# Stage one of two sequences with the two parts of x as rows, other ticks for the transforms, and two loads cut in the passage

## The chip, the cores and the metric

The kernel runs on one core of one Trainium2 chip. The metric is the device time of one execution in microseconds (us), smaller is better. The kernel before takes 1383.81 us, the median of three runs (1381.85 to 1385.62).

The names of the engines: PE is TensorE (PEld its weight loads), DVE is VectorE, ACT is ScalarE, POOL is GpSimd, SP is SyncE, which here only issues DMAs. Each engine runs its own instructions strictly in the order in which they stand.

## The reference

x has 4 sequences of 3008 rows of 256 columns. The Fourier transform runs along the 3008.

```python
X = np.fft.rfft(x, axis=1)
Yr = X.real @ w_r - X.imag @ w_i + b_r
Yi = X.real @ w_i + X.imag @ w_r + b_i
Yr = np.sign(Yr) * np.maximum(np.abs(Yr) - 0.01, 0.0)      # Yi likewise
y = np.fft.irfft(Yr + 1j * Yi, n=3008, axis=1)
h = y.reshape(12032, 256) @ w_in                           # 256 -> 2048
g = h / (1.0 + np.exp(-h))                                 # h * sigmoid(h)
out = g @ w_out                                            # 2048 -> 256
```

## The kernel before

3008 is 47 times 64, so each transform is two short ones. *Stage one* (`s1...`) takes 47 points: x is read as 94 rows by 32 columns of D=256, a row p being n2 and the upper or lower half of n1 together (p = 2·n2 + half), and a table of 94 x 96 is multiplied with it. Its result goes to a scratch tensor in DRAM (`scr1`). *Stage two* (`s2`, `s2_3`) takes the 64 points, then come the mix with w_r and w_i (`mix`, `mix3`, `shrink`), the first inverse stage (`split_z`, `i1`), a second scratch tensor (`scr2`), its reload (`g_load`, tile `gin`), and the second inverse stage (`i2`, `i2_ends`), which writes `xt`, the input of the MLP. The MLP's tokens go in 24 blocks (23 of 512 and one of 256).

A product of full precision is made of three products of the type fp32r, which holds fewer bits: a value is split into a high part (a cast on ACT) and a low part (value minus high part, on DVE), and high·high, high·low and low·high are added in PSUM. So stage one of the third and fourth sequence (`s1_half`, line 225) has three products of 512 columns for each half of a group of 1024 columns, and 8 groups for each sequence.

The first sequence, stage one of the second, and part of the splitting of w_in and w_out run ahead of the MLP: the *prologue*. Its last part, from the last inverse stage of sequence one to the first MLP products, is called the *passage* here. Then follow 384 *ticks*, one for each block and each 128 of the 2048 inner columns. Tick t issues, in this order: the split of the previous tick's g (`split_g`: ACT L512, DVE L513), a deferred `shrink`, the first product of tick t (`mlp1`: six matmuls, L495; then ACT sigmoid L502 and DVE product L503), then whatever was put into tick t (`fill`), then DMA stores, then the second product of tick t-2 (`mlp2`: eight matmuls, L535 and L539). The ticks 0 to 7 belong to block 0, 8 to 23 to block 1.

What is put where is decided when the program is written out: `put(t, ...)` takes the first free tick from t on, and `at(t, ...)` any tick. Stage two to i1 of a sequence is cut into pieces (`u3_step`), which take their ticks first, then stage one takes what is free. `W_GO[t]` is the number of steps that tick t does on the splitting of the MLP's weights; there are three kinds of step, which follow one another: two DVE operations L597 and L598, two DVE operations L604 and L605 (with ACT L601 and the beginning of the next weight, L595), two DVE operations L608 and L609. A split of x (`s1_split`) is put with `at`, its product with `put` in a later tick.

In the table below a tile's name is written without its number; `x_sb` and `x_pre` hold x, `sx` its split, `s1o` stage one's result, `d` is a pair of PSUM banks that all the products of the fills share in turn.

Of the kernel before, what the change touches and what calls it, by code (L numbers as in the profile page):

```python
# [100 lines left out]
def spectral_mlp_kernel(ctx: ExitStack, tc: tile.TileContext, x, w_r, w_i, b_r, b_i, w_in, w_out, c1, c2, c3, c4, c3f, out):  # L101
# [110 lines left out]
    def s1_split(b, g, i):  # L212
        t = x_t[b, g][:NP, i * 512:(i + 1) * 512]
        sx = sb.tile([128, 2, 512], F32R, tag="sx", bufs=1, name="sx")
        nc.scalar.copy(sx[:NP, 0, :], t)
        nc.vector.tensor_sub(sx[:NP, 1, :], t, sx[:NP, 0, :])  # L216
        x_t[b, g, i] = sx

    def s1_half(b, g, i):
        sx = x_t.pop((b, g, i))  # L220
        if i == 0:
            x_t[b, g, "o"] = sb.tile([128, 4 * D], F32, tag="s1o", bufs=2, name="s1o")[:96, :]
        o = x_t[b, g, "o"]
        p = bank("s1")
        s1_product(p, (sx[:, 0, :], sx[:, 1, :]))
        nc.scalar.copy(o[:, i * 512:(i + 1) * 512], p[:96, :])
        if i == 0:
            s1_split(b, g, 1)
        else:
            v = scr1[b].rearrange("r (a j) d -> (r a) (j d)", a=4)  # L230
            store(v[:, g * 4 * D:(g + 1) * 4 * D], o)
            del x_t[b, g], x_t[b, g, "o"]
            x_ahead()
# [617 lines left out]
```

## Time and profile before

| | |
|---|---|
| median of the runs | 1383.81 us |
| the profiled execution | 1383.51 us |
| its span, from first to last instruction | 1381.5 us |
| mean granted clock of TensorE | 0.998 |
| busy: TensorE, VectorE, ScalarE, GpSimd | 99%, 64%, 51%, 7% of the span |
| TensorE idle on the chain of waits | 4 steps over 1 us: 3.7 and 3.0 us on loads, 1.7 us on a load, 1.3 us on VectorE |

A step of the chain of waits names the instruction that waited and what came last before it could run. TensorE's rows overlap one another, since matmuls are pipelined: what one costs is the distance from its start to the start of the next, not its duration.

### The profile page before, as it was taken

Reading aid. Unit: us, or ns where it says so; the run is one execution under the profiler, and the core shown is the slowest. Engines: PE = TensorE matmul, PEld = TensorE weight load, DVE = VectorE, ACT = ScalarE, POOL = GpSimd, SP = SyncE. Lnnn points to the kernel's source line nnn. Section 1 sums busy time; section 2 is a strip of 40 time slices with the busy share of each in tenths; the row PEclk is TensorE's granted clock in tenths of the full one; section 3 lists DMA queues with packets and bytes.
Section 4 is the critical chain, followed back from the end, with each engine's and each line's share of the span. In section 5 each row is a group of like instructions: output and inputs, shape, how many; then the busy total and the mean of one; then the engine's idle time right before and its main releaser. Section 6 shows DMA issues by size and latency. Waiting matters only on the chain.

```text
span 1381.5 us, 20358 instructions
## 1 busy us (share of the span) xinstructions
PE 1363.3 (99%) x7621; PEld 1168.3 (85%) x7621; DVE 888.2 (64%) x1517; ACT 705.5 (51%) x1386; POOL 98.8 (7%) x145
## 2 busy tenths in 40 slices
PE   8998999999999999999999999999999999999998
PEld 4976788888888888888888888888888888888888
DVE  3867979687655677767655577776654555455555
ACT  5445555555564555555454445454454444444444
POOL 2000012111000101111100011111000000000000
PEclk9999999999999999999999999999999999999999
DMA  8874334231423214333121022220210110011001
GB/s 263 268 226 144 93 88 119 76 97 32 123 76 101 58 43 107 89 94 81 50 73 54 20 77 60 75 81 25 61 32 12 27 39 10 18 27 39 0 16 24
DMA packets 69932, 103.51 MB, mean 75 GB/s; under 512 B 7306, under 2 KB 53002, under 8 KB 69834
## 3 DMA queue, kind: packets, MB, share of 16 engines
q1 hardware_dynamic: 58163, 79.07, 19.8%
q0 software_dynamic: 8096, 19.45, 5.4%
q10 hardware_dynamic: 3575, 3.70, 0.8%
q8 instruction: 60, 0.98, 0.3%
q14 instruction: 38, 0.31, 0.1%
HBM read 64.70 MB, written 37.49 MB: 74 GB/s over the span
## 4 chain that ended last, share of the span: by engine, by line
PE 94%; DMA 2%; DVE 2%; ACT 1%; issue 1%; SPq 0%; ACTq 0%; DVEq 0%
PE h L495 37%; PE acc L535 24%; PE acc L539 12%; PE mix L349 6%; PE i L438 3%; PE s L324 2%; PE mix L288 2%; PE s L173 2%; PE i L397 2%; PE s L189 1%; PE acc L530 1%; PE s L267 1%; PE i L394 1%; PE i2e L438 1%; DMA t3f<-in_c3f_dram 1%
## 5 line engine op out<-in xcount | busy, mean ns | idle before, releaser
L495 PE MATMUL h<-xt,win 128*128 128x512 f32 (+1 forms) x2304 | 585.5, 389 | 0.4 <-DVE g L503 0.2
L535 PE MATMUL acc<-wout,gh 128*128 128x512 f32 x1472 | 540.7, 401 | 0.0
L495 PEld LDWEIGHTS h<-xt,win 128*128 128x128 f32 x2304 | 401.7, 188 | 82.7 <-ACT xt L454 0.5
L502 ACT ACTIVATE g<-h 128x512 f32<-128x512 f32 (+1 forms) x385 | 226.1, 587 | 385.0 <-PE h L495 384.1
L503 DVE TENSOR_TENSOR g<-h,g 128x512 f32<-128x512 f32 (+1 forms) x385 | 261.0, 678 | 239.8 <-ACT g L502 236.5
L539 PE MATMUL acc<-wout,gl 128*128 128x256 f32 x1472 | 413.1, 281 | 1.3 <-DVE gl L513 1.3
L513 DVE TENSOR_TENSOR gl<-g,gh 128x512 fp32r<-128x512 f32 (+1 forms) x385 | 276.0, 717 | 169.2 <-ACT gh L512 165.0
L535 PEld LDWEIGHTS acc<-wout,gh 128*128 128x128 f32 x1472 | 277.6, 189 | 59.4 <-issue 0.5
L512 ACT CAST gh<-g 128x512 fp32r<-128x512 f32 (+1 forms) x385 | 235.3, 611 | 158.5 <-DVE g L503 155.9
L539 PEld LDWEIGHTS acc<-wout,gl 128*128 128x128 f32 x1472 | 278.6, 189 | 11.5 <-DVE gl L513 2.4
L356 POOL TENSOR_TENSOR q<-q,bias 128x256 f32<-128x256 f32 x36 | 26.4, 733 | 652.6 <-ACT q L355 652.6
L438 PEld LDWEIGHTS i<-c_sb,gin 96*128 96x128 f32 x420 | 54.9, 193 | 8.6 <-issue 4.3
L369 DVE TENSOR_TENSOR y<-q,mix 64x256 f32<-64x256 f32 x144 | 60.3, 419 | 2.2
L438 PE MATMUL i<-c_sb,gin 96*128 96x94 f32 x420 | 54.2, 274 | 3.3 <-DMA gin<-scr 3.3
L324 PEld LDWEIGHTS s<-t,a 128*128 128x128 f32 x288 | 37.7, 191 | 3.0
L324 PE MATMUL s<-t,a 128*128 128x128 f32 x288 | 37.9, 275 | 0.0
L455 DVE TENSOR_TENSOR xt<-i,xt 128x376 fp32r<-128x376 f32 (+2 forms) x48 | 28.0, 583 | 12.4 <-ACT xt L454 6.7
L173 PE MATMUL s<-sx,c 94*96 94x512 f32 (+1 forms) x111 | 34.1, 414 | 0.2 <-DVE sx L216 0.2
L397 PE MATMUL i<-zh,t 128*128 128x256 f32 x144 | 33.7, 297 | 0.0
L401 ACT COPY i1o<-i 128x512 f32<-128x512 f32 x48 | 27.8, 580 | 10.2 <-PE i L394 9.0
L556 DVE TENSOR_TENSOR o<-acc,o 128x256 f32<-128x256 f32 x92 | 32.6, 413 | 0.0
L357 POOL TENSOR_TENSOR q<-q,bias 128x256 f32<-128x256 f32 x36 | 31.9, 886 | 2.8
(118 smaller groups left out, 1164.7 us busy)
## 6 DMA issues: line engine op xcount, KB each, us to landing
a<-scr SPq DMA_DIRECT2D x48, 256.0 KB
gin<-scr SPq DMA_DIRECT2D x32, 384.0 KB
scr<-s1o SPq DMA_DIRECT2D x31, 384.0 KB
t<-in_c_dram POOLq DMA_DIRECT2D x36, 256.0 KB, 3.0
scr<-i1o SPq DMA_DIRECT2D x36, 256.0 KB
x_sb<-in_x_dram POOLq DMA_DIRECT2D x22, 376.0 KB, 4.1
t<-in_c_dram SPq DMA_DIRECT2D x48, 128.0 KB
w<-in_moe_w_in_dram SPq DMA_DIRECT2D x8, 512.0 KB
```

The source lines that it names most:

```text
L173: nc.tensor.matmul(out=p[:96, :], lhsT=c1_hl[m][:K, :], rhs=hl[k][:K, :], start=(n == 0), stop=(n == 2))
L324: nc.tensor.matmul(out=pv[:, e, :, r, :], lhsT=a[:, r, e * 128:(e + 1) * 128], rhs=t2[:, r * 128:(r + 1) * 128], start=True, stop=True,)
L349: nc.tensor.matmul(out=out, lhsT=x_[:, e, c, :], rhs=m[:, e, :], start=(n == 0), stop=(n == 5))
L397: nc.tensor.matmul(out=pv[:, r, :], lhsT=t3[:, m, q], rhs=z[k][:, r, :], start=(n == 0), stop=(n == 2),)
L438: nc.tensor.matmul(out=p[:, o:o + m], lhsT=g_t[b, j // 4][:, q:q + 128], rhs=c4_sb[:, p0:p0 + m], start=True, stop=True,)
L495: nc.tensor.matmul(out=p[:, :n], lhsT=w[:, e, f * 128:(f + 1) * 128], rhs=v[:, e, :n], start=(m == 0), stop=(m == 5),)
L502: nc.scalar.activation(out=g[:, q], in_=p[:, q], func=ACTF.Sigmoid)
L503: nc.vector.tensor_tensor(out=g[:, q], in0=p[:, q], in1=g[:, q], op=ALU.mult)
L512: nc.scalar.copy(gh[:, q], g[:, q])
L513: nc.vector.tensor_sub(gl[:, q], g[:, q], gh[:, q])
L535: nc.tensor.matmul(out=a, lhsT=gh[:, q], rhs=wout[:, f].rearrange("p a c -> p (a c)"), start=begins, stop=False,)
L539: nc.tensor.matmul(out=a[:, D:2 * D], lhsT=gl[:, q], rhs=wout[:, f, 0, :], start=False, stop=ends,)
```

## The change

Stage one of the sequences 2 and 3 (the third and fourth) is done another way. The two halves of n1 are taken apart, so that a piece of x has 47 rows (n2) and not 94, and there are 16 groups for each sequence and not 8. A piece is loaded twice, to the rows 0 to 46 and to the rows 64 to 110 of the same tile. The high part is cast over all 111 rows, and the rows from 64 on are replaced by the low part, so the two parts of x are rows of one operand. The new table c5 has its high part in the columns 0 to 63 and its low part in the columns 64 to 127, at both row ranges. One product then gives rows 0 to 63, the table's high part times both parts of x, and rows 64 to 127, the table's low part times both; ACT copies 48 of the lower rows out, and DVE adds the upper ones.

GpSimd loads c5 at tick 30, and the 64 loads of x where it issued 16. The splits and products get other ticks (third sequence from 54 on, every 2.8 ticks; fourth from 114 on, every 4.4), and so do the pieces of stage two to i1 (third from tick 104 every 4.3 instead of 92 every 5, fourth from 190 every 4.8 instead of 186 every 5). The last two products of stage one of the second sequence (`s1_later(7, ...)`) move from the ticks 2 and 4 to 6 and 7. `W_GO` does 13 steps in the ticks 0 to 7 where it did 11, the same as before in the ticks 8 to 18, and 5 instead of 7 after; the sum is 30 both times.

In the passage, the two loads of `gin` for block 0 are cut: 88 rows of each are issued one step of the pipeline earlier, after i1's last result but one, and 8 rows after the last one. The results of stage one for groups 4 and 5 of the second sequence go to two x tiles that nothing needs any more (later block 1's `xt`), so they don't wait for the two `s1o` buffers.

```diff
-W_GO = [2, 1, 1, 2, 1, 1, 2, 1, 0, 0, 0, 2, 1, 2, 1, 2, 1, 2, 1, 1, 2, 1, 2, 1]
+W_GO = [2, 2, 1, 2, 1, 2, 2, 1, 0, 0, 0, 2, 1, 2, 1, 2, 1, 2, 1, 2, 1, 1, 1]
...
+    def x_load_twice(b, q):
+        t = x_sb[q % 2]
+        if b == STACKED and q < 2:
+            nc.gpsimd.memset(t[32:64, :], 0.0)
+        h, g = divmod(q, 8)
+        v = x[b].rearrange("(n h j) d -> n h (j d)", h=2, j=NJ)[:, h, g * 4 * D:(g + 1) * 4 * D]
+        for p in (0, 64):
+            nc.gpsimd.dma_start(out=t[p:p + RR, :], in_=v)
+        return t
...
-    def s1_split(b, g, i):
...
-    def s1_half(b, g, i):
...
+    def stack_split(b, q):
+        t = x_t[b, q]
+        sx = sb.tile([128, 4 * D], F32R, tag="sx", bufs=1, name="sx")
+        nc.scalar.copy(sx[:64 + RR, :], t[:64 + RR, :])
+        nc.vector.tensor_sub(sx[64:64 + RR, :], t[64:64 + RR, :], sx[64:64 + RR, :])
+        x_t[b, q] = sx
+
+    def stack_product(b, q):
+        sx = x_t.pop((b, q))
+        o = sb.tile([128, 4 * D], F32, tag="s1o", bufs=2, name="s1o")[:2 * NR, :]
+        for i in range(2):
+            p = bank("s1")
+            c = slice(i * 512, (i + 1) * 512)
+            nc.tensor.matmul(out=p, lhsT=c5_sb[:64 + RR, :], rhs=sx[:64 + RR, c], start=True, stop=True)
+            nc.scalar.copy(o[:, c], p[64:64 + 2 * NR, :])
+            nc.vector.tensor_tensor(out=o[:, c], in0=p[:2 * NR, :], in1=o[:, c], op=ALU.add)
+        h, g = divmod(q, 8)
+        v = scr1[b].rearrange("r (i h j) d -> (r i) h (j d)", i=2, h=2)
+        store(v[:, h, g * 4 * D:(g + 1) * 4 * D], o)
+        x_ahead()
...
         s1(1, 2, late=True)
+        for g in range(2):
+            loaded.add((0, g))
+            g_load(0, g, slice(0, 88))
         flush(1)
         u_step(NU + 1)
         s1(1, 3, late=True)
-        i2_load(0)
-        flush(1)
+        for g in range(2):
+            g_load(0, g, slice(88, 96))
         s1(1, 4, late=True)
...
-            put(2, s1_later, 7, i)
+            put(5, s1_later, 7, i)
...
-        for b, t0, dt in ((2, 37, 6), (3, 110, 8)):
+        for b, t0, dt in ((2, 54, 2.8), (3, 114, 4.4)):
             t = 0
-            for g in range(8):
-                t = max(t, t0 + dt * g)
-                at(t, s1_split, b, g, 0)
-                t = put(t + 1, s1_half, b, g, 0)
-                t = put(t + 1, s1_half, b, g, 1)
+            for q in range(16):
+                t = max(t, int(t0 + dt * q))
+                at(t, stack_split, b, q)
+                t = put(t + 1, stack_product, b, q)
```

Three places where the order moves. First ScalarE in two ticks on end in stage one of the third sequence; before, one tick with a product and the split for the next one (`gh` begins a tick, the sigmoid `g` follows it):

```order
L512 CAST gh<-g 128x512 [waits DVE_49]
L502 ACTIVATE g<-h 128x512 [waits PE_49,Activation_49]
L226 COPY s1o<-s_2416 96x512 [waits PE_49]
L215 CAST sx<-x_sb_69 94x512 [waits DVE_49]
L512 CAST gh<-g 128x512 [waits DVE_49]
```

And in the changed kernel two such ticks on end, the ticks 68 and 69:

```order
L540 CAST gh<-g 128x512 [waits DVE_49]
L530 ACTIVATE g<-h 128x512 [waits PE_49,Activation_49]
L255 COPY s1o<-s_3725 48x512 [waits PE_49]
L255 COPY s1o<-s_3729 48x512 [waits PE_49]
L244 CAST sx<-x_sb_69 111x1024 [waits DMASW4_49,DMASW3_49,Activation_49]
L540 CAST gh<-g 128x512 [waits DVE_49]
L530 ACTIVATE g<-h 128x512 [waits PE_49,Activation_49]
L255 COPY s1o<-s_3765 48x512 [waits DMAHW7_49,PE_49]
L255 COPY s1o<-s_3769 48x512 [waits PE_49]
L244 CAST sx<-x_sb_70 111x1024 [waits DMASW6_49,DMASW5_49,DVE_49]
```

Between the sigmoid and the next `gh` stand three instructions where there were two, and the cast is of 1024 columns and not of 512. The product of the next tick needs this cast, and VectorE's subtraction behind it.

Second, TensorE in the ticks 1 and 2 (`i` is the second inverse stage of block 1, `h` mlp1, `acc` mlp2, `s` stage one). Before:

```order
L438 MATMUL i_1091<-c_sb,gin 128x94
L495 MATMUL h<-xt_1013,win_79 128x512 [waits DVE_49]
L495 MATMUL h<-xt_1013,win_80 128x512
L495 MATMUL h<-xt_1014,win_79 128x512
...
L205 MATMUL s_1123<-x_sb_69,c_sb 96x512 [waits DMAHW4_49,DMAHW3_49,PE_49]
L535 MATMUL acc<-wout,gh 128x512 [waits Activation_49]
L539 MATMUL acc<-wout,gl 128x256 [waits DVE_49]
```

In the changed kernel:

```order
L466 MATMUL i_1092<-c_sb,gin 128x94
L523 MATMUL h<-xt_1014,win_80 128x512 [waits DVE_49]
L523 MATMUL h<-xt_1014,win_81 128x512
L523 MATMUL h<-xt_1015,win_80 128x512
...
L563 MATMUL acc<-wout,gh 128x512 [waits Activation_49]
L567 MATMUL acc<-wout,gl 128x256 [waits DVE_49]
```

The product `s`, which waits for a load of x, is gone from tick 2 (it stands in tick 6), so mlp2 follows mlp1 and waits for VectorE's `gl` alone.

Third, SyncE's queue in the passage. Before:

```order
L142 DMA scr_1_83<-s1o 96x1024 [waits DMAHW0_49,Activation_49]
L409 DMA gin<-scr_0_86 96x1024 [waits DMAHW4_49,DMAHW2_49,DMAHW7_49,DMAHW1_49,DVE_49]
L409 DMA gin<-scr_0_86 96x1024 [waits DMAHW3_49,DVE_49]
L142 DMA scr_1_83<-s1o 96x1024 [waits Activation_49]
L579 DMA w_999<-in_moe_w_out_dram 128x2x512 [waits DMAHW5_49,DVE_49]
L142 DMA scr_1_83<-s1o 96x1024 [waits DMAHW6_49,Activation_49]
```

In the changed kernel:

```order
L438 DMA gin<-scr_0_87 88x1024 [waits DMAHW4_49,DMAHW0_49,DMAHW7_49,DVE_49,Activation_49]
L438 DMA gin<-scr_0_87 88x1024 [waits DMAHW2_49,DVE_49,Activation_49]
L157 DMA scr_1_84<-s1o 96x1024 [waits DMAHW3_49,Activation_49]
L438 DMA gin<-scr_0_87 8x1024 [waits DMAHW1_49]
L438 DMA gin<-scr_0_87 8x1024 [waits DMAHW5_49]
L607 DMA w_1000<-in_moe_w_out_dram 128x2x512 [waits DMAHW6_49,DVE_49]
L157 DMA scr_1_84<-s1o 96x1024 [waits Activation_49]
L157 DMA scr_1_84<-x_pre 96x1024 [waits DMAHW0_49,DMASW5_49,Activation_49]
```

The long loads stand ahead of a store of 96 rows, the two short ones behind it; two stores of stage one come behind the weights' load where one stood ahead of it.

## Rows read from the trace of the kernel before

**Rows 1.** The page's first part: busy us, share of span, instructions.

```profile
PE 1363.3 (99%) x7621; PEld 1168.3 (85%) x7621; DVE 888.2 (64%) x1517; ACT 705.5 (51%) x1386; POOL 98.8 (7%) x145
```

**Rows 2.** Windows: length, busy us (instructions) by engine, PE's granted clock, DMA share, GB/s.

```profile
95.00:98.50 3.50, 0.48 (x4) 0.39 (x4) 0.95 (x2) 0.12 (x1) 0.00 (x0) 1.00 0.91 263
98.50:102.00 3.50, 3.50 (x14) 2.41 (x14) 0.41 (x1) 1.52 (x3) 0.00 (x0) 0.53 0.80 316
...
111.00:115.50 4.50, 0.83 (x4) 0.43 (x3) 4.07 (x8) 2.29 (x4) 0.00 (x0) 1.00 0.47 111
115.50:119.50 4.00, 4.00 (x13) 3.21 (x12) 2.49 (x4) 1.10 (x2) 0.00 (x0) 0.57 0.39 132
...
181.00:700.00 519.00, 518.48 (x2985) 450.97 (x2984) 361.74 (x627) 281.72 (x565) 61.97 (x90) 1.00 0.29 81
```

**Rows 3.** Timeline of two ticks: start us, us, engine, line, operation [idle before].

```profile
522.99 0.86 PE L173 MATMUL s<-sx,c 94*96 94x512 f32 x3
...
523.69 0.40 PE L535 MATMUL acc<-wout,gh 128*128 128x512 f32 x1
...
525.08 1.55 PE L495 MATMUL h<-xt,win 128*128 128x512 f32 x6
...
526.47 0.39 PE L535 MATMUL acc<-wout,gh 128*128 128x512 f32 x1
...
526.73 0.60 ACT L502 ACTIVATE g<-h 128x512 f32<-128x512 f32 x1 [0.87 <-PE h L495]
...
527.36 0.69 DVE L503 TENSOR_TENSOR g<-h,g 128x512 f32<-128x512 f32 x1 [0.78 <-ACT g L502]
...
527.86 1.55 PE L495 MATMUL h<-xt,win 128*128 128x512 f32 x6
```

**Rows 4.** Timeline of a tick with a split of x, ScalarE.

```profile
533.92 0.60 ACT L502 ACTIVATE g<-h 128x512 f32<-128x512 f32 x1 [0.30 <-PE h L495]
...
534.42 0.61 ACT L215 CAST sx<-x_sb 94x512 fp32r<-94x512 f32 x1
```

**Rows 5.** Groups by shape, ScalarE: count, busy us, mean ns, idle before.

```profile
L226 ACT COPY s1o<-s 96x512 f32<-96x512 f32 x32 | 18.6, 582 | 2.5 <-PE s L173 0.5
...
L623 ACT ACTIVATE x_pre<-x_pre 64x1024 uint32<-64x1024 uint32 x2 | 2.0, 1036 | 0.0
```

**Rows 6.** Groups by shape, VectorE.

```profile
L216 DVE TENSOR_TENSOR sx<-x_sb,sx 94x512 fp32r<-94x512 f32 x32 | 22.4, 699 | 10.2 <-ACT sx L215 10.0
...
L503 DVE TENSOR_TENSOR g<-h,g 128x256 f32<-128x256 f32 x15 | 6.4, 424 | 2.2 <-ACT g L502 0.7
```

**Rows 7.** Who ScalarE's L475 (end of `i2_ends`) waits for: us, times.

```profile
  DVE xt L473: 20.1, 23
```

**Rows 8.** Timeline of the passage and the ticks 0 to 2.

```profile
90.62 0.37 ACTq L138 DMA_DIRECT2D scr<-i1o  x1
...
93.57 0.80 SPq L409 DMA_DIRECT2D gin<-scr  x2
...
98.14 1.27 PE L438 MATMUL i<-c_sb,gin 96*128 96x94 f32 x7 [3.02 <-DMA gin<-scr]
...
108.64 0.69 DVE L503 TENSOR_TENSOR g<-h,g 128x512 f32<-128x512 f32 x1 [0.58 <-ACT g L502]
...
109.25 0.68 DVE L608 TENSOR_TENSOR ww<-ww,wout 128x512 f32<-128x512 f32 x1
...
110.58 0.42 DVE L597 TENSOR_SCALAR ww<-ww 128x512 uint32<-128x512 uint32 x1
...
111.64 0.68 DVE L513 TENSOR_TENSOR gl<-g,gh 128x512 fp32r<-128x512 f32 x1
...
114.73 1.07 PE L205 MATMUL s<-x_sb,c_sb 128*96 128x512 f32 x2 [3.67 <-DMA x_sb<-in_x_dram]
...
115.23 0.91 PE L535 MATMUL acc<-wout,gh 128*128 128x512 f32 x1
```

**Rows 9.** Timeline, TensorE at the start of tick 11.

```profile
143.01 1.32 PE L495 MATMUL h<-xt,win 128*128 128x512 f32 x5
```

**Rows 10.** Loads of x issued by GpSimd (L158, 376 KB each).

```profile
DMA to landing us min/median/max: 3.5/4.8/10.8
```

More of the change, by code (lines that the diff above doesn't have):

```diff
@@ L90, in dft_tables @@
     c3f = c3
+    c, s = trig(np.outer(n2, r), RR)
+    c5 = np.zeros((128, 2, KK))
+    c5[:RR, 0, :2 * NR] = np.stack([c, -s], axis=2).reshape(RR, 2 * NR)
+    c5[:, :, 1] = 0.0
+    c5 = c5.astype(np.float32)
+    bits = c5[:RR, 0].view(np.uint32).astype(np.uint64)
+    c5h = ((bits + 0x7FF + ((bits >> 12) & 1)) & 0xFFFFF000).astype(np.uint32).view(np.float32)
+    c5[:RR, 1] = c5[:RR, 0] - c5h
+    c5[:RR, 0] = c5h
+    c5[64:64 + RR] = c5[:RR]
     return {
@@ L96, in dft_tables, with spectral_mlp_kernel @@
         "c3f": c3f,
+        "c5": c5.reshape(128, 128),
     }
 @with_exitstack
-def spectral_mlp_kernel(ctx: ExitStack, tc: tile.TileContext, x, w_r, w_i, b_r, b_i, w_in, w_out, c1, c2, c3, c4, c3f, out):
+def spectral_mlp_kernel(ctx: ExitStack, tc: tile.TileContext, x, w_r, w_i, b_r, b_i, w_in, w_out, c1, c2, c3, c4, c3f, c5, out):
     nc = tc.nc
@@ L111, in spectral_mlp_kernel @@
     c4_sb = cst.tile([96, NP], F32, name="c4_sb")
+    c5_sb = cst.tile([128, 128], F32R, name="c5_sb")
     bias = cst.tile([128, 2, D], F32, name="bias")
@@ L159, in x_load @@
         return t
-    x_next = [(b, g) for b in range(NB) for g in range(8)]
+    def x_load_twice(b, q):
[7 more added lines that the diff above has]
+        return t
+    x_next = [(b, g) for b in range(NB) for g in range(16 if b >= STACKED else 8)]
     def x_ahead():
@@ L165, in x_ahead @@
             q = x_next.pop(0)
-            x_t[q] = x_load(*q)
+            x_t[q] = (x_load_twice if q[0] >= STACKED else x_load)(*q)
     x_t = {}
@@ L176, in s1 @@
         t = x_t.pop((b, g))
-        tag, bufs = ("s1o", 2) if 8 * b + g in (6, 7, 10, 11, 12, 13) else ("gin", 4)
-        o = sb.tile([128, 4 * D], F32, tag=tag, bufs=bufs, name="s1o")[:96, :]
+        if b == 1 and g in (4, 5):
+            o = x_pre[g + 1][:96, :]
+        else:
+            tag, bufs = ("s1o", 2) if 8 * b + g in (6, 7, 10, 11) else ("gin", 4)
+            o = sb.tile([128, 4 * D], F32, tag=tag, bufs=bufs, name="s1o")[:96, :]
         for i in range(2):
@@ L210, in s1_later @@
             del x_t[1, g], x_t[1, g, "o"]
-    def s1_split(b, g, i):
[L213 to L217, printed above, removed]
-    def s1_half(b, g, i):
[L220 to L233, printed above, removed]
+    def stack_split(b, q):
[17 more added lines that the diff above has]
+        x_ahead()
     u_t = {}
@@ L404, in spectral_mlp_kernel, with g_load @@
     g_t = {}
-    def g_load(b, g):
-        t = sb.tile([96, 4 * D], F32, tag="gin", bufs=4, name="gin")
+    def g_load(b, g, rows=slice(0, 96)):
+        if (b, g) not in g_t:
+            g_t[b, g] = sb.tile([96, 4 * D], F32, tag="gin", bufs=4, name="gin")
         v = scr2[b].rearrange("r (a j) d -> (r a) (j d)", a=4)
-        nc.sync.dma_start(out=t, in_=v[:, g * 4 * D:(g + 1) * 4 * D])
-        g_t[b, g] = t
+        nc.sync.dma_start(out=g_t[b, g][rows, :], in_=v[rows, g * 4 * D:(g + 1) * 4 * D])
     def pieces(c0, n):
@@ L744, in spectral_mlp_kernel @@
         s1(1, 5, late=True)
-        flush(1)
+        flush(2)
         w_go()
@@ L793, in spectral_mlp_kernel @@
         t = 13
-        for b, t0, dt in ((1, t + 11, 3.1), (2, 92, 5), (3, 186, 5)):
+        for b, t0, dt in ((1, t + 11, 3.1), (2, 104, 4.3), (3, 190, 4.8)):
             at(t0 - 2, u_load, b, 0)
```

2 lines of the change are left out of this document (added).

## The prediction

> **What bounds the kernel now.** I read the page's busy shares first, then windows, then timelines of single ticks. TensorE is busy 99% of the span, VectorE 64%, ScalarE 51% [rows 1], so only what TensorE issues or waits for can move the time. From 181 to 700 us it is busy 518.48 of 519.00 us at full clock [rows 2]: no wait is left there to remove, only work, and every new wait is a loss. A bare tick is 2.78 us, from the start of one mlp1 to the next, 1.39 of it mlp1 [rows 3]. TensorE's idle time lies in the passage: 3.02 us on the load of gin and 3.67 us on a load of x [rows 8]. After each the granted clock falls to about half, the lower of its two levels: 0.53 over 3.5 us and 0.57 over 4.0 us [rows 2], which costs 3.5·0.47 = 1.6 and 4.0·0.43 = 1.7 us of work.
>
> **Term 1, products.** A half costs TensorE 523.69 - 522.99 = 0.70 us for three matmuls of 512 columns, and mlp1 525.08 to 526.47 = 1.39 for six [rows 3]: 0.232 each by both. 1024 columns of x take six such matmuls now and four in the new form (two products for each of two pieces of half the rows), so 96 become 64 in all: 32·0.232 = 7.4 us less. It lies wholly on the path. If the change of operand is part of the 0.70, the remaining ones cost it too, and the gain is smaller: 6.4 with 0.20 for a bare matmul.
>
> **Term 2, the passage.** (a) SyncE issues gin at 93.57, once i1's last store, issued at 90.62, has landed, and TensorE begins at 98.14 after 3.02 us of idling [rows 8]. Now 88 rows go about 3 us earlier, and only 8 rows wait for that store. These can still queue behind the long loads and a store of 384 KB; at the 263 GB/s of this stretch [rows 2] such 1.1 MB take 4.2 us from about 91, so I expect the last rows near 96.5: 1.6 us earlier (0 to 3.0). With half the idling the clock may stay up: 1.6 us with a chance of about 0.6, so 1.0. Together 2.6 (0 to 4.6).
>
> (b) The product that waits for x moves from tick 2 to ticks 6 and 7, by which time its load is long there. The wait doesn't fall to zero: mlp2 of tick 2 needs gl, which VectorE begins at 111.64 and has at 112.32, behind two steps of the weights [rows 8]. So TensorE, which starts it at 115.23, could start it at 112.37, and the clock wouldn't fall. Next VectorE is late. From g at 108.64 on, g and gl take 0.61 each, the step at 109.25 1.33, those of two L597-like operations 111.64 - 110.58 = 1.06 [rows 8]. Ticks 0 to 7 now hold 8·1.22 - 0.61 for g and gl, 1.4 for block 1's xt, 5·1.33 + 8·1.06 for the 13 steps: 25.7 us, and the next gl is done at 26.3; mlp2 of tick 9 (1.39) and tick 10 (2.78) put tick 11's start 30.5 after that g, if VectorE never idles. TensorE's own work comes to 3.7 + 1.39 + 8·2.78 and some 3.0 of fills, 30.3. Today it is 143.01 - 108.64 = 34.4 [rows 8, 9]. With 0.8 us for casts that VectorE waits for, the gain is 3.1 (1.0 to 4.1). The two steps that come earlier cost VectorE about 2.3 here; they are gone from behind tick 18, where I give nothing for it. The ticks 11 to 18 keep their number of steps, and I carry the gain over them unchanged.
>
> (a) and (b) make 5.7 (1 to 8.7). A cover of (b) is that the weights' loads arrive in time for steps that follow closer; each that is late takes some tenths off.
>
> **Term 3, new waits.** ScalarE's sigmoid begins 526.73 - 526.47 = 0.26 us after TensorE has gone on from mlp1 [rows 3], the next ScalarE instruction 0.50 later [rows 4]. The new cast has 1024 columns: 1.04 us by the only row of that width [rows 5]. VectorE follows 0.03 behind (526.73 + 0.60 to 527.36, rows 3); its subtraction of 1024 columns is 0.70 + 2·0.275 = 1.25, from 699 ns at 512 and 424 at 256 [rows 6]; 0.05 to TensorE. Sum: 0.26 + 0.50 + 1.04 + 0.03 + 1.25 + 0.05 = 3.13. The product stands in the next tick behind its mlp1, and TensorE is there after 2.78: it waits 0.35. Before, for halves, the same chain with 512 columns is 0.26 + 0.50 + 0.62 + 0.03 + 0.70 + 0.05 = 2.16, and no wait.
>
> By the table of ticks this is so, with nothing else put into the split's tick, for the products in 80, 83, 85, 88, 167, 176 and 181: 7·0.35 = 2.4. In 69 to 72, 133 and 163 the split's tick also holds the product before it, and its two copies of 0.50 come ahead of the cast: 4.13 against 2.78 + 0.46, a wait of 0.89. After such a wait the sigmoid is already done and the chain 0.25 shorter, so 70, 71 and 72 wait 0.6: together 3·0.89 + 3·0.6 = 4.5. In tick 93 the split stands behind i2_ends, whose last copy waits 20.1/23 = 0.87 for VectorE [rows 7]: about 1.2 in 94, and 0.2 in 172 behind i2. In 115 and 150 the mix in the split's tick (18 matmuls of 256 columns, 18·0.116 = 2.1) covers it; without that cover it would be 0.35 each. Sum 8.3 us. The bounds: below 0 nothing can go, and 0 would need ScalarE's cast ahead of the sigmoid, which its order forbids; 0.2 less for each of the 15 waits makes 5.3, 0.25 more 12.
>
> The rest is costed at nothing. ScalarE gets 32·(1.04 + 2·0.58) - 32·(0.61 + 0.58) = 32 us more [rows 4, 5], VectorE 32·(1.25 + 1.40) - 32·0.70 = 62 us more: covered while a tick's sum stays under TensorE's, and in 68 to 72 VectorE has 2·0.61 + 2·0.61 + 1.25 = 3.7 in ticks that the waits above make 3.8 and longer. GpSimd's 48 more loads stand ahead of its additions for mix3, about 1.1 us in a slack of a tick. Stage two's denser ticks are no denser than those of the second sequence, which run without a wait.
>
> **Sum.** The profiled execution took 1383.5 us (2.0 outside its span), 0.3 under the median. 1383.5 - 7.4 - 5.7 + 8.3 = 1378.7; I say 1379.0.
>
> **The rivals.** *The waits of term 3 are absorbed* (casts and subtractions overlap better than I add them): 1383.5 - 7.4 - 5.7 = 1370.4, with a quarter of them 1372.5. For it: VectorE idles a third of the time. Against: both engines run in order, and the chain starts at the sigmoid.
>
> *The passage gives nothing*: the short loads land with the long ones and the two extra steps make VectorE late for every tick up to 8, so (b) gives 1 and (a) none: 1383.5 - 7.4 - 1 + 8.3 = 1383.4. For it: the DMA share is 0.91 in that stretch [rows 2]. The Trainium skill (DMA: Bandwidth & Descriptors, Rules for kernel authors) says of two transfers to disjoint halves of the partitions that they serialize and should be one. No run here shows two such loads yet; by that rule the cut gains only what the earlier issue gives, and (a) would be near its lower end.
>
> *The x loads come late* (the slower end). A piece has 47 rows, a prime. If such a load ran on one DMA engine, its 192 KB would take, at 316 GB/s over a share of 0.80·16 = 24.7 GB/s an engine [rows 2], 7.8 us, about 9 with issue, in place of 3.5 to 4.8 [rows 10]. In the ticks 68 to 78 a buffer comes free only about 6 us before ScalarE's cast needs its next x; ScalarE, in order, would hold gh and the sigmoid behind it. Price: some 2 to 2.5 us for each of four reloads there and one at 162, +10, so 1389. It decides from a landing time of about 6 us on. The loads of 94 rows, which have no divisor up to 16 but 2, land in 3.5 us at best [rows 10], half of what two engines would need, and that speaks against it. The Trainium skill (DMA: Bandwidth & Descriptors, Why a DMA increments its semaphore by 16 and not by 1) says that the number of engines is the largest up to 16 that divides the row count, with some GpSimd copies excepted; the trace puts the 94 rows among the exceptions, and shows no 47.
>
> **How the numbers follow.** About 0.3%, 4.15 us, is what a measurement of this kernel can tell from no change: faster is below 1379.7, slower above 1388.0. Forecast, 1376 to 1382: 0.42, of which 0.27 falls under 1379.7 and 0.15 in between. Waits absorbed: 0.22, all faster. Passage gives nothing: 0.24, all the same. Late loads: 0.12, 0.11 of it slower. So faster 0.49, same 0.40, slower 0.11. The range of 1371 to 1387 leaves out about 2 in 10, most of it late loads.
>
> **What would show it.** Stage one of the two sequences has 64 matmuls on TensorE. In the list of waits TensorE's product of sx waits for VectorE's subtraction some 15 times, 0.3 to 1.2 us each, 8 in all; if it's under 3, term 3 is wrong. The wait for x before L205 is gone, and the start of tick 11 stands 5 to 7 us earlier, at 136 to 138; if it is at 141 or later, term 2 is. The wait for gin is nearer 1.5 than 3. Loads of x by GpSimd land within 5 us; if ScalarE's cast waits for them in the third sequence, the slower rival holds. A clock under 1.00 anywhere behind 125 us would contradict all of it.

## The result, and the profile after

The changed kernel takes 1393.72 us (median of 8 runs, 1390.42 to 1400.5), the kernel before 1382.96 beside it: a ratio of 1.008, 95% interval 1.0065 to 1.0096, slower by about 11 us. The forecast was 1379.0, faster, and the time lies outside its range. The profiled execution took 1394.55, of which 1392.7 are its span, against 1381.5 before.

The first part of the page after, beside [rows 1], and its chain of waits by engine:

```profile
PE 1362.9 (98%) x7589; PEld 1162.8 (83%) x7589; DVE 940.7 (68%) x1581; ACT 731.4 (53%) x1418; POOL 123.4 (9%) x196
...
PE 86%; DVE 5%; DMA 3%; ACT 3%; issue 2%; SPq 0%; ACTq 0%; DVEq 0%
```

The chain before:

```profile
PE 94%; DMA 2%; DVE 2%; ACT 1%; issue 1%; SPq 0%; ACTq 0%; DVEq 0%
```

TensorE has its 32 matmuls less, and yet the span is longer: more of the path that sets the end now runs over VectorE, ScalarE and DMAs. Where TensorE waits, over the whole program (us in total, times, longest):

```profile
PE s L254 <- DVE sx L245: 7.0, 14, 1.1
PE i L466 <- DMA gin<-scr: 5.6, 2, 4.7
PE acc L567 <- DVE gl L541: 3.3, 6, 1.5
PE s L254 <- DVE y L396: 2.6, 2, 1.3
```

And before:

```profile
PE s L205 <- DMA x_sb<-in_x_dram: 3.7, 1, 3.7
PE i L438 <- DMA gin<-scr: 3.3, 2, 3.0
...
PE acc L539 <- DVE gl L513: 1.3, 1, 1.3
```

The wait for x is gone. Three places are new or wait longer, and each answers to one term of the prediction. L254 is the new product of stage one, L466 the first use of `gin` in the passage, L567 the part of mlp2 that needs `gl`. These lists take idle time from the modelled end of the matmul before, which lies behind the point where the next could have begun; by the distances between starts, the waits in front of L254 come to 12.9 us.

To see how much belongs to each place, I cut both executions at the starts of mlp1 of the ticks 0, 11 and 24. TensorE in the changed kernel at these three points:

```profile
108.36 0.94 PE L523 MATMUL h<-xt,win 128*128 128x512 f32 x3
...
144.59 0.86 PE L523 MATMUL h<-xt,win 128*128 128x512 f32 x3
...
185.32 0.86 PE L523 MATMUL h<-xt,win 128*128 128x512 f32 x3
```

Before, the second of these starts is 143.01 [rows 9], and the other two are:

```profile
104.14 0.70 PE L495 MATMUL h<-xt,win 128*128 128x512 f32 x2
...
181.04 1.09 PE L495 MATMUL h<-xt,win 128*128 128x512 f32 x4
```

So the passage ends 4.2 us later, the ticks 0 to 24 take the same time to 0.1 us (76.96 against 76.90), and what follows takes 6.9 us more (1207.38 against 1200.46). The prediction had -2.6, -3.1 and +0.9 there.

Each of these figures is of one execution, and the traces of the experiments below show how far one can be trusted. Behind tick 24 the eight kernels that keep stage one as it was take 1200.46 to 1200.65 us, so the 6.9 are firm. So is the stretch from tick 11 to 24: 38.0 to 38.1 us in the ten kernels with the old `W_GO`. The passage and the first ticks scatter. Where that part of the program is as before, tick 0 starts between 100.8 and 107.2, and the ticks 0 to 11 take 36.6 to 40.1; in part this is TensorE's granted clock, which falls there in one execution and not in another (over 3.5 us from the first use of `gin` on it is 0.50 in the changed kernel, and 1.00 in the kernel with the product alone). The 4.2 and the 0.1 are therefore not shown by these two traces. For the front part I go by medians, and by distances that repeat.

### The profile page after: what moved, and what is told of

The parts are those of the page before. It is cut to its first block, busy times and chain, and to the rows that moved or that the text cites. A ratio compares the mean times of both kernels' runs of the same rounds, so it can differ in the third digit from the quotient of the medians.

```text
span 1392.7 us, 20595 instructions
## 1 busy us (share of the span) xinstructions
PE 1362.9 (98%) x7589; PEld 1162.8 (83%) x7589; DVE 940.7 (68%) x1581; ACT 731.4 (53%) x1418; POOL 123.4 (9%) x196
## 4 chain that ended last, share of the span: by engine, by line
PE 86%; DVE 5%; DMA 3%; ACT 3%; issue 2%; SPq 0%; ACTq 0%; DVEq 0%
PE h L523 34%; PE acc L563 22%; PE acc L567 11%; PE mix L376 5%; PE i L466 3%; PE s L351 2%; PE i L424 2%; PE mix L315 2%; DVE sx L245 1%; PE s L254 1%; ACT sx L244 1%; DVE gl L541 1%; DMA scr<-s1o 1%; PE acc L558 1%; DMA scr<-i1o 1%
## 5 line engine op out<-in xcount | busy, mean ns | idle before, releaser
L567 PE MATMUL acc<-wout,gl 128*128 128x256 f32 x1472 | 413.0, 281 | 3.4 <-DVE gl L541 3.3
L567 PEld LDWEIGHTS acc<-wout,gl 128*128 128x128 f32 x1472 | 278.3, 189 | 15.3 <-DVE gl L541 6.0
L383 POOL TENSOR_TENSOR q<-q,bias 128x256 f32<-128x256 f32 x36 | 26.4, 732 | 558.8 <-ACT q L382 558.8
L466 PEld LDWEIGHTS i<-c_sb,gin 96*128 96x128 f32 x420 | 55.7, 195 | 11.5 <-issue 6.0
L466 PE MATMUL i<-c_sb,gin 96*128 96x94 f32 x420 | 54.8, 276 | 5.6 <-DMA gin<-scr 5.6
L245 DVE TENSOR_TENSOR sx<-x_sb,sx 47x1024 fp32r<-47x1024 f32 x32 | 40.7, 1271 | 10.7 <-ACT sx L244 9.7
L184 POOL DMA_DIRECT2D x_sb<-in_x_dram x64 | 32.6, 511 | 154.2 <-ACT sx L244 135.0
L256 DVE TENSOR_TENSOR s1o<-s,s1o 48x512 f32<-48x512 f32 x64 | 40.8, 675 | 0.0
L351 PEld LDWEIGHTS s<-t,a 128*128 128x128 f32 x288 | 37.7, 191 | 3.0
L483 DVE TENSOR_TENSOR xt<-i,xt 128x376 fp32r<-128x376 f32 (+2 forms) x48 | 28.0, 584 | 14.7 <-ACT xt L482 14.7
L255 ACT COPY s1o<-s 48x512 f32<-48x512 f32 x64 | 34.3, 582 | 6.3 <-PE s L254 4.9
L244 ACT CAST sx<-x_sb 111x1024 fp32r<-111x1024 f32 x32 | 33.5, 1047 | 1.5 <-DMA x_sb<-in_x_dram 1.5
```

Source lines behind the costliest of these rows:

```text
L245: nc.vector.tensor_sub(sx[64:64 + RR, :], t[64:64 + RR, :], sx[64:64 + RR, :])
L351: nc.tensor.matmul(out=pv[:, e, :, r, :], lhsT=a[:, r, e * 128:(e + 1) * 128], rhs=t2[:, r * 128:(r + 1) * 128], start=True, stop=True,)
L466: nc.tensor.matmul(out=p[:, o:o + m], lhsT=g_t[b, j // 4][:, q:q + 128], rhs=c4_sb[:, p0:p0 + m], start=True, stop=True,)
L567: nc.tensor.matmul(out=a[:, D:2 * D], lhsT=gl[:, q], rhs=wout[:, f, 0, :], start=False, stop=ends,)
```

## The experiments

Twelve kernels ran, each timed in 5 rounds against the kernel before on the same chip. Four of them hold a part of the change by itself: stage one, the transforms' ticks, the loads, and the later product with the new order of the steps. In the code `...` marks lines left out.

**Only stage one.** The kernel after, with the rest of the change taken back, except for the transforms' ticks.

```diff
-W_GO = [2, 2, 1, 2, 1, 2, 2, 1, 0, 0, 0, 2, 1, 2, 1, 2, 1, 2, 1, 2, 1, 1, 1]
+W_GO = [2, 1, 1, 2, 1, 1, 2, 1, 0, 0, 0, 2, 1, 2, 1, 2, 1, 2, 1, 1, 2, 1, 2, 1]
...
-        for g in range(2):
-            loaded.add((0, g))
-            g_load(0, g, slice(0, 88))
...
-        for g in range(2):
-            g_load(0, g, slice(88, 96))
+        i2_load(0)
+        flush(1)
...
-            put(5, s1_later, 7, i)
+            put(2, s1_later, 7, i)
```

> The kernel after with the passage, the weights' steps and the product that waits for x put back as before: the stacked first stage of the third and fourth sequence and the moved transforms are what is left of the change. Theory W (the waits of TensorE for split and evictions cost 12.9 us, 32 fewer matmuls give 7.4): about 5.5 to 6 us over before, 1388 to 1390, with the same 19 waits in front of the products. Rival P (most of the loss after the passage is a follow-up of the late passage): level with before or up to 5 us under it, 1378 to 1384.

Measured 1389.63 us against 1383.01, ratio 1.0051 (1.0036 to 1.0066): +6.6. Theory W holds, P falls: the loss behind the passage is stage one's own.

**Two ticks.**

```diff
-                t = put(t + 1, stack_product, b, q)
+                t = put(t + 2, stack_product, b, q)
```

> The same, with every product two ticks behind its split instead of one; as many instructions. Theory W: the waits go (under 1.5 us of them left), so the 7.4 us of the 32 missing matmuls come out: 1375 to 1378. Rival M (a product of 111 rows, its operand change or the bank it writes costs TensorE more than the matmuls that are gone): level with before or over it, 1382 to 1388.

Measured 1376.52 us, ratio 0.996 (0.9945 to 0.9975): 6.5 under before, 13.1 under the kernel with one tick. From tick 24 to the end, first the kernel with stage one alone (windows: length, then busy us and instructions of TensorE, its weight loads, VectorE, ScalarE, GpSimd):

```profile
182.79:1391.60 1208.81, 1193.05 (x6710) 1032.04 (x6708) 813.13 (x1366) 636.73 (x1236) 109.64 (x173) 1.00 0.23 61
```

Then the same with two ticks:

```profile
179.34:1372.70 1193.36, 1188.41 (x6710) 1033.26 (x6708) 812.10 (x1366) 636.18 (x1236) 109.57 (x173) 1.00 0.23 62
```

And the kernel before:

```profile
181.04:1381.50 1200.46, 1195.88 (x6742) 1037.49 (x6740) 760.23 (x1302) 609.94 (x1204) 85.71 (x124) 1.00 0.21 57
```

The same instructions, 6710 on TensorE in both, take 15.5 us less when the product waits a tick longer. (The medians give 13.1, each with an interval of about 2 us either way. The stretch itself repeats: 1193.36 to 1193.42 in the three kernels with two ticks.) In its list of waits no product is left. Against before 7.1 us are gained, with 0.4 us of small waits still in: the 7.4 us of 32 matmuls. VectorE and ScalarE have 52 and 26 us more to do than before there, and it costs nothing.

**Split in halves.** Stage one alone, with the product one tick behind.

```diff
-        nc.scalar.copy(sx[:64 + RR, :], t[:64 + RR, :])
-        nc.vector.tensor_sub(sx[64:64 + RR, :], t[64:64 + RR, :], sx[64:64 + RR, :])
+        for i in range(2):
+            c = slice(i * 512, (i + 1) * 512)
+            nc.scalar.copy(sx[:64 + RR, c], t[:64 + RR, c])
+            nc.vector.tensor_sub(sx[64:64 + RR, c], t[64:64 + RR, c], sx[64:64 + RR, c])
```

> The kernel of the first run (stacked first stage alone, product one tick behind its split), with the split in two halves of 512 columns: cast, subtraction, cast, subtraction. ScalarE and VectorE have slightly more to do, but the chain ends about 0.6 us earlier, since the second cast runs beside the first subtraction. Theory W (the length of the chain from the sigmoid decides): the seven plain waits of 0.35 go, those of 0.6 to 1.3 shrink by about 0.5, 3 to 5 us of 12.9 are left, 1380 to 1384. Rival T (VectorE's total of work in a tick decides): no shorter waits, 1388 to 1391.

Measured 1386.0 us against 1383.23, ratio 1.002 (1.0007 to 1.0034), between W's range and T's. The list of waits:

```profile
PE s L253 <- ACT s1o L254: 2.2, 2, 1.1
PE s L253 <- DVE sx L244: 1.4, 3, 0.6
```

By starts the waits fall from about 14 to about 8 us, and the seven plain ones are gone, so the chain's length decides and rival T falls. I had expected 3 to 5 us left: behind a tick that also holds a product, the second half still comes 0.35 late, which I had not counted.

**Only the transforms' ticks.** The kernel before, with:

```diff
-        for b, t0, dt in ((1, t + 11, 3.1), (2, 92, 5), (3, 186, 5)):
+        for b, t0, dt in ((1, t + 11, 3.1), (2, 104, 4.3), (3, 190, 4.8)):
```

> The kernel before with only the new starts and spacings of the transforms of the third and fourth sequence. Theory W: their ticks stay under TensorE's length in either place, 1382 to 1384. Rival U (part of the loss behind tick 24 is theirs): 1385 or more.

Measured 1383.13 us against 1383.23, ratio 1.0 (0.9985 to 1.0014). Behind tick 24 its profiled execution takes 1200.46 us, as before. They cost nothing; U falls.

**Only the loads of the passage.** The kernel before with the two cut loads, the stores behind them and the two outputs in x tiles, as the change has them.

```diff
...
         s1(1, 2, late=True)
+        for g in range(2):
+            loaded.add((0, g))
+            g_load(0, g, slice(0, 88))
         flush(1)
         u_step(NU + 1)
         s1(1, 3, late=True)
-        i2_load(0)
-        flush(1)
+        for g in range(2):
+            g_load(0, g, slice(88, 96))
...
```

> The kernel before with only the passage's loads of the change: gin in 88 and 8 rows, the stores behind them, two outputs kept in x_pre. Theory Q (the early loads stand in front of the last store of i1o and of a store of s1o on the DMA engines, so the 8 rows are issued 5 us later than the whole load was): tick 0 starts 4 us later, total 1386 to 1389, the last store of i1o lands over 6 us after its issue against 2.95 before. Rival L (the passage is late in the changed kernel for another reason, such as the moved steps of the weights): tick 0 within 1 us of before, total 1380 to 1384.

Measured 1386.14 us against 1383.01, ratio 1.0022 (1.0013 to 1.0032): +3.1, just inside Q's range. Tick 0 starts 2.6 us later than before and not 4. Such starts scatter, though: i1o's last store is issued at 91.59 in the changed kernel, at 90.62 before [rows 8], and anywhere from 88.30 to 93.70 in the kernels whose passage is as before. Counted from this store tick 0 begins 16.4 us behind it here and 16.8 in the changed kernel, against 13.5 before. SyncE in this kernel:

```profile
89.85 0.73 SPq L414 DMA_DIRECT2D gin<-scr  x2
90.67 0.31 SPq L142 DMA_DIRECT2D scr<-s1o  x1
97.46 0.60 SPq L414 DMA_DIRECT2D gin<-scr  x2
```

The last store of i1o is issued at 90.34; the loads of 8 rows, which wait for it, at 97.46, 7.1 us later. Before it was 2.95 [rows 8], and 2.92 to 2.96 in the eight other kernels whose passage is as before. Theory Q holds.

**Store ahead.** The same, with the first store back in front of the loads of 88 rows.

```diff
         s1(1, 2, late=True)
+        flush(1)
         for g in range(2):
             loaded.add((0, g))
             g_load(0, g, slice(0, 88))
-        flush(1)
```

> The kernel of the third run (the passage's loads alone), with the store of s1o issued before the loads of 88 rows, as it stood before the change. Theory Q1 (half of the loss is SyncE: the s1o store stands behind a load that waits, and its 384 KB then run beside i1o's last store): i1o's last store lands about 5 us after its issue in place of 7.1, 1384 to 1385.3. Rival Q2 (the 704 KB of the early loads alone hold that store up): the landing stays at 6.5 us or more, 1386 to 1387.5.

Measured 1383.68 us against 1383.23, ratio 1.0 (0.9985 to 1.0016). SyncE, with i1o's last store issued at 88.87:

```profile
87.88 0.33 SPq L142 DMA_DIRECT2D scr<-s1o  x1
88.38 6.36 SPq L414 DMA_DIRECT2D gin<-scr  x4
```

The 8 rows now go 5.3 us behind that store, as Q1 said, and the time is just under Q1's range. TensorE begins at 96.32, 7.45 behind the store; before it was 7.52. So the place of the other store was the loss, and cutting the load gains nothing. The Trainium skill (DMA: Bandwidth & Descriptors, Rules for kernel authors) says not to bother with two transfers to disjoint halves; the trace agrees, with 0.07 us between the two.

**Two ticks, stores behind.** Of the passage's edits only the order and the two outputs in x tiles: `gin` whole, once i1o has landed, and the three stores of stage one after it. The difference from the kernel with two ticks:

```diff
...
         s1(1, 2, late=True)
-        flush(1)
         u_step(NU + 1)
         s1(1, 3, late=True)
         i2_load(0)
-        flush(1)
...
         s1(1, 5, late=True)
-        flush(1)
+        flush(3)
```

> The kernel with products two ticks behind their split, and of the passage's edits only the order of the stores: gin is loaded whole, once i1o has landed, and all three stores of s1o follow it. Theory Q (what stands in front of i1o's last store on the DMA engines sets when gin is loaded): the 384 KB in front of it are gone, it lands 1 to 1.4 us earlier, gin with it: 1374.5 to 1376. If the cut into 88 and 8 rows were not what cost the time, but the stores behind it: later than the kernel without it, 1378 to 1380.

Measured 1374.56 us against 1383.23, ratio 0.9939 (0.9918 to 0.996). The interval reaches that of the kernel without the edit, so the time alone doesn't tell them apart; the trace does:

```profile
95.76 1.55 PE L466 MATMUL i<-c_sb,gin 96*128 96x94 f32 x10 [1.59 <-DMA gin<-scr]
```

i1o's last store, issued at 89.67, lands in 2.25 us, and TensorE begins 6.1 us behind it in place of 7.5, with 1.59 us idle in place of 3.02 [rows 8]. All passages side by side, each from the issue of i1o's last store, in us (the kernel of the last row is the last experiment below):

| kernel | to the load that waits for it | to TensorE's first use of `gin` | to tick 0 |
|---|---|---|---|
| before | 2.95 | 7.5 | 13.5 |
| eight others with this passage | 2.92 to 2.96 | 6.7 to 7.5 | 12.3 to 14.7 |
| the kernel after | 7.14 | 9.2 | 16.8 |
| only the loads | 7.12 | 9.4 | 16.4 |
| store ahead | 5.27 | 7.5 | 13.5 |
| two ticks, stores behind | 2.25 | 6.1 | 12.3 |
| what beats both | 2.24 | 6.3 | 12.6 |

**Only the later product.** The kernel before, with:

```diff
-W_GO = [2, 1, 1, 2, 1, 1, 2, 1, 0, 0, 0, 2, 1, 2, 1, 2, 1, 2, 1, 1, 2, 1, 2, 1]
+W_GO = [2, 2, 1, 2, 1, 2, 2, 1, 0, 0, 0, 2, 1, 2, 1, 2, 1, 2, 1, 2, 1, 1, 1]
...
-            put(2, s1_later, 7, i)
+            put(5, s1_later, 7, i)
```

> The kernel before with only the product that waits for x moved from tick 2 to ticks 6 and 7, and the new order of the weights' steps. Theory V (VectorE holds the ticks 3 to 21 in either order, so what is gained up to tick 11 is given back): tick 11 2 to 3 us earlier, tick 24 within 0.7 us of before, total 1382.5 to 1384. Rival F (the gain stays where the passage is not late, as predicted): tick 24 3 us earlier, total 1379 to 1380.5.

Measured 1383.38 us against 1383.01, ratio 1.0006 (0.9996 to 1.0016). The time is as V says, but a time that is as expected doesn't show why. The next kernel showed that V was false.

**The product alone.** Of that difference only the second part, with the old `W_GO`.

> The kernel before with the product that waits for x in ticks 6 and 7, and the weights' steps in their old order. Theory V (VectorE has no idle time to give between ticks 3 and 21, whoever takes the steps): the 3 us are back by tick 24, total 1382.3 to 1384. Rival F (the two steps that the new order takes forward eat the gain): TensorE keeps 1.5 to 3 us at tick 24, total 1380 to 1381.7.

Measured 1379.51 us against 1382.3, ratio 0.9978 (0.9966 to 0.999): -2.8, a little under F's range. V falls and F holds: VectorE has room for it, and the new order of the steps eats the gain. A difference is in ScalarE. Its waits for `ww` in the ticks 9 to 23, in the kernel with both:

```profile
ACT wout L601 <- DVE ww L598: 6.8, 3, 2.5
ACT win L601 <- DVE ww L598: 4.9, 2, 2.5
```

And with the old order:

```profile
ACT wout L601 <- DVE ww L598: 1.2, 1, 1.2
```

Which steps share a tick decides these waits. VectorE makes `ww` in step A, ScalarE casts it in B, VectorE ends in C; a tick with two steps holds B and C in the old order, and A and B in the new one, from tick 11 to 19. What runs in TensorE's tick 17 of the changed kernel (lines picked from the timeline):

```profile
160.81 0.42 DVE L625 TENSOR_SCALAR ww<-ww 128x512 uint32<-128x512 uint32 x1
161.26 0.69 DVE L626 SCALAR_TENSOR_TENSOR ww<-w,ww 128x512 uint32<-128x512 uint32 x1
161.70 2.83 POOL L339 TENSOR_TENSOR w32d<-w 128x512 f32<-128x512 f32 x2 [25.23 <-DMA w<-in_w_i_dram]
161.99 0.62 ACT L629 CAST win<-ww 128x512 fp32r<-128x512 f32 x1 [2.47 <-DVE ww L626]
161.99 1.41 DVE L632 TENSOR_SCALAR we<-ww 128x512 uint32<-128x512 uint32 x1
163.08 0.60 ACT L540 CAST gh<-g 128x512 fp32r<-128x512 f32 x1
163.43 1.64 DVE L633 SCALAR_TENSOR_TENSOR we<-w,we 128x512 f32<-128x512 uint32 x1
165.00 0.68 DVE L541 TENSOR_TENSOR gl<-g,gh 128x512 fp32r<-128x512 f32 x1
165.73 0.39 PE L567 MATMUL acc<-wout,gl 128*128 128x256 f32 x1 [1.50 <-DVE gl L541]
```

Read it from the top: the cast waits 2.47 us for VectorE's two instructions of the same tick; `gh` stands behind the cast, `gl` needs `gh`, and by then VectorE has begun the next two, so TensorE waits 1.5 us.

Most of this 1.5 is not the pairing's. Two additions of GpSimd run in this tick, and beside them VectorE's L632 and L633 take 1.41 and 1.64 us. In tick 15, with the same pairing and no GpSimd, they are short:

```profile
155.32 0.43 DVE L632 TENSOR_SCALAR we<-ww 128x512 uint32<-128x512 uint32 x1
...
155.79 0.69 DVE L633 SCALAR_TENSOR_TENSOR we<-w,we 128x512 f32<-128x512 uint32 x1
...
157.82 0.39 PE L567 MATMUL acc<-wout,gl 128*128 128x256 f32 x1 [0.22 <-DVE gl L541]
```

Before the change TensorE waited in the same tick too, behind the same additions:

```profile
162.79 0.39 PE L539 MATMUL acc<-wout,gl 128*128 128x256 f32 x1 [1.28 <-DVE gl L513]
```

What the pairing adds is seen from the lengths of the ticks, from one mlp1 to the next: 15, 17, 19 and 21 are longer than before by 0.56, 0.80, 0.81 and 0.53 us, 2.7 together, and the other nine of the ticks 11 to 23 are not.

**One step more, and the order alone.** Two kernels to part the pairing from the steps taken early. The second is the kernel before with the new `W_GO` and nothing else; the first has, beside the kernel with the product and the new order:

```diff
-W_GO = [2, 2, 1, 2, 1, 2, 2, 1, 0, 0, 0, 2, 1, 2, 1, 2, 1, 2, 1, 2, 1, 1, 1]
+W_GO = [2, 2, 1, 2, 1, 2, 2, 2, 0, 0, 0, 2, 1, 2, 1, 2, 1, 2, 1, 2, 1, 1, 1]
```

> The kernel of the fourth run (product for x in ticks 6 and 7, new order of the weights' steps) with one step more in tick 7 and one fewer at the end. Each weight takes three steps: A (VectorE makes ww), B (ScalarE casts it, VectorE goes on), C (VectorE ends). In the new order the five ticks 11, 13, 15, 17 and 19 hold A and B, so ScalarE's cast waits about 2.5 us for an A of the same tick, with gh and so gl and mlp2 behind it; in the old order they held B and C. With one step more before them they hold B and C again, while three instead of two steps are taken earlier than in the old order. Theory N (which steps share a tick decides): ScalarE waits for ww under 9 us in place of 16.7, total 1379 to 1381.5. Rival F (the steps taken earlier cost it, whatever their pairing): 1383 or more.

> The kernel before with the new order of the weights' steps and nothing else (the product that waits for x stays in tick 2). Theory N: ScalarE's waits for ww in the ticks 11 to 19 come without any gain against them, 2.5 to 4 us: 1385 to 1387. If the new order only costs where the product is moved (VectorE late because TensorE is early): 1382.5 to 1384.

Measured 1383.13 us against 1383.32, ratio 0.9995 (0.9985 to 1.0004), for the first, and 1386.69, ratio 1.0025 (1.0015 to 1.0034), for the second. The order alone costs 3.4, as N says. The first misses N's range and lies in F's, and the starts of mlp1 say why (us from the start of one tick to that of another, one execution each; the ticks 0 to 11 scatter, as said above; the other two columns repeat, with 8.4 and 38.0 to 38.1 in all ten kernels with the old order):

| kernel | 0 to 11 | of it 8 to 11 | 11 to 24 |
|---|---|---|---|
| before | 38.9 | 8.4 | 38.0 |
| the product alone | 35.9 | 8.4 | 38.1 |
| product and new order | 37.4 | 9.2 | 40.9 |
| product, new order, one step more | 37.7 | 10.4 | 38.3 |
| new order alone | 39.3 | 8.8 | 40.8 |
| the kernel after | 36.2 | 9.3 | 40.7 |

Both theories hold a part. The pairing costs 2.7 us in the ticks 11 to 24, by the last two rows, and one step more takes that away but for 0.3: ScalarE waits for `ww` there not once. (The 40.9 of the third row isn't clean: the granted clock is 0.96 there, and 1.00 in the others.) The steps taken early cost 0.4 to 0.9 us in the ticks 8 to 10 when they are two, and 2.0 when they are three; what more they cost ahead of tick 8 a single execution doesn't show.

**What beats both.** Two ticks, stores behind, and the product in the ticks 6 and 7 with the old `W_GO`.

> The kernel with products two ticks behind their split and the stores behind the whole load of gin, and that product in ticks 6 and 7 with the old order of the weights' steps. By theory V as fast as without the move, 1374 to 1376; by rival F 1.5 to 3 us faster, 1371.5 to 1373.

Measured 1371.35 us against 1382.3, ratio 0.9921 (0.9901 to 0.9941), 11 us faster than before. That lies just under F's range: the 2.8 us of the product's move add to the rest.

## Why the prediction was wrong

**Term 1, the products (-7.4), was right.** It measures -7.1 once the waits are gone, and TensorE's busy time behind tick 24 falls by 1195.88 - 1188.41 = 7.47.

**Term 2 (a), the loads (-2.6), is the step that failed most.** I saw that the last rows could queue behind the long loads and put them at 96.5, from 1.1 MB at 263 GB/s. But I let the wrong transfer queue. The 8 rows can't be issued before i1o's last store has landed, and that store now runs beside 704 KB of `gin` and the 384 KB of s1o that SyncE, held by a load that waits, had let go only behind them. By the kernel with the loads alone this costs 3.1 us, in place of a gain of 2.6. SyncE in the changed kernel:

```profile
91.10 0.72 SPq L438 DMA_DIRECT2D gin<-scr  x2
91.92 0.31 SPq L157 DMA_DIRECT2D scr<-s1o  x1
98.73 0.60 SPq L438 DMA_DIRECT2D gin<-scr  x2
```

Its windows, with the DMA share and GB/s at the end of a row:

```profile
92.00:98.00 6.00, 4.09 (x10) 1.30 (x8) 1.38 (x2) 4.38 (x8) 0.00 (x0) 1.00 0.77 229
98.00:100.70 2.70, 0.00 (x0) 0.00 (x0) 0.00 (x0) 0.00 (x0) 0.00 (x0) 0.99 0.12 36
100.70:104.20 3.50, 3.43 (x12) 2.87 (x13) 0.39 (x1) 0.55 (x1) 0.00 (x0) 0.50 0.83 303
104.20:108.40 4.20, 4.20 (x18) 2.62 (x16) 0.50 (x2) 1.64 (x4) 0.00 (x0) 0.61 0.14 53
```

6 us of transfers at 229 GB/s are 1.37 MB, the 1344 KB that stand together there; only then come the 8 rows, and for 2.7 us nearly nothing moves but them. TensorE idles 4.68 us, not the 1.5 I named as the sign, and the clock behind it is granted at 0.50, the lower of its two levels, where it was 0.53 [rows 2], and stays low longer. The clock's share can't be told from one execution, and the 1.0 us that I gave for it rested on a link with the length of the idling that the runs don't bear out. In the kernel with the product alone TensorE idled nearly as long as before, and the clock stayed up:

```profile
97.19 0.99 PE L438 MATMUL i<-c_sb,gin 96*128 96x94 f32 x7 [2.63 <-DMA gin<-scr]
...
97.19:100.69 3.50, 3.49 (x18) 2.36 (x19) 0.00 (x0) 1.40 (x3) 0.00 (x0) 1.00 0.98 362
```

With the stores behind, it idled 1.59, and the clock was 0.73 over the 3.5 us that follow. In the rest of the term I had counted bytes; the order of what waits for what was missing from the count. The Trainium skill (DMA: Bandwidth & Descriptors, Issuing engines are not separate DMA queues) says that the DMAs of all engines run on the same 16 DMA engines and interleave. The trace agrees: ScalarE's store slowed from 2.95 to 7.1 us by transfers that SyncE issued.

**Term 2 (b), the moved product (-3.1), was right, and the steps that moved with it were not.** Alone the move gives -2.8. "The ticks 11 to 18 keep their number of steps, and I carry the gain over them unchanged" is the sentence that failed: the number stayed, the pairing changed. In the changed kernel tick 11 starts at 144.59, behind the 141 I had named as the sign, and from there to tick 24 the pairing costs 2.7 us, about what the move gives. The product and the new order together measure +0.4. I had read ScalarE's casts as covered and never asked which of VectorE's steps each one waits for.

**Term 3, the waits (+8.3), was mis-sized: 12.9.** The list shows 16 where I named 15, and the starts show one more. The plain ones are as worked out, seven of 0.31 to 0.42 against 0.35; so are those of the ticks 70 to 72 (0.58 to 0.60 against 0.6) and of 94 (1.27 against 1.2). Two sorts were not. (The rest is tick 69, 1.05 against 0.89, and two small ones in 120 and 132, 0.4 together, which the kernel with two ticks keeps.) In 133 and 163 the wait is 1.3 and not 0.89, since VectorE's two additions of the product (0.675 each) stand ahead of the subtraction. And in 115 and 150 I took the mix in the split's tick for a cover. It covers TensorE's time, but its results load VectorE. The ticks 114 and 115:

```profile
518.96 0.74 POOL L384 TENSOR_TENSOR q<-q,bias 128x256 f32<-128x256 f32 x1
519.04 1.74 DVE L245 TENSOR_TENSOR sx<-x_sb,sx 47x1024 fp32r<-47x1024 f32 x1 [0.73 <-ACT sx L244]
520.81 0.69 DVE L541 TENSOR_TENSOR gl<-g,gh 128x512 fp32r<-128x512 f32 x1
521.52 1.72 DVE L396 TENSOR_TENSOR y<-q,mix 64x256 f32<-64x256 f32 x4
521.68 0.40 PE L254 MATMUL s<-sx,c_sb 111*128 111x512 f32 x1
523.38 0.47 PE L254 MATMUL s<-sx,c_sb 111*128 111x512 f32 x1 [1.30 <-DVE y L396]
```

The first half of the product runs on time. The second waits for VectorE to read the mix's results, which stand behind the subtraction and `gl`: by starts 1.47 us, twice. About 0.5 of it is the subtraction's own, which takes 1.74 us beside GpSimd and not 1.22 (last section).

**What the waits and the rest add up to.** 1383.5 - 7.4 + 3.1 + 0.4 + 12.9 = 1392.5, with the time of the product and the new order together for (b); measured are 1394.55 in the profiled execution and 1393.72 in the median. That the sum comes near is in part luck: its two middle terms are medians with intervals of over 1 us either way.

**The rivals.** None of them came. The waits were not absorbed. The passage gave less than nothing. The loads of x don't come late: they land in a median of 3.5 us (7.4 at most), and ScalarE's cast waits for x once, 1.5 us. The granted clock is 1.00 in the mean from 125 us to the end, as I had said. The slower side was reached by a way that I had put into the range of no term: the gains of (a) and (b) were bounded by 0 and 1.0 below, though no row showed a cut load or the new pairing, and the waits by 12 above.

## What to carry to other kernels

A load that is issued earlier also stands earlier in front of everything else; before moving it, list what its last piece waits for, and whether that now runs beside the load itself. When work for two engines is given out in steps, look at which steps share a tick and not only at how many there are. And a producer in the tick before its user has the length of a tick for its whole chain, on every engine that it crosses, with what those engines do first: one tick more cost nothing here and was worth 13 us. When two traces are compared, find out first which stretches repeat from execution to execution; here those from tick 8 on did, and the passage and the first ticks did not.

## What the runs showed of the hardware

VectorE's subtraction of 1024 columns takes 1.22 us where GpSimd adds nothing and 1.74 beside GpSimd's additions, as above (the line gives the shortest, the median and the longest):

```profile
L245 DVE TENSOR_TENSOR sx<-x_sb,sx x32: 1221/1222/1741, 311.6 to 767.5; 47x1024 fp32r<-47x1024 f32 x32
```

The same holds in tick 17, where L632 takes 1.41 us beside GpSimd and not the 0.43 of tick 15. The Trainium skill (SBUF — State Buffer, SBUF: two separate sides) says that the two engines share one pair of ports by a lock that the loser waits for; the 1.74 agrees, since the subtraction begins while an addition of 0.74 runs that has 0.66 left, and is longer by 0.52.
